# Value products of a sliding-window attention on eight TensorE tiles in place of four lanes

## The chip, the cores and the metric

The kernel runs on one core of one Trainium2 chip. The metric is the device time of one execution in microseconds (us), as the median of several runs.

## The reference

The input x has 2048 rows of 640 numbers. It is normalised (layer norm) and then used twice.

```python
qkv = (xn @ wqkv)                      # 32 heads of 20 numbers each
scores = q k^T * 20 ** -0.5            # key j counts for query i if 0 <= i - j < 256
p = softmax(scores);  o = p v
s = o @ wo
h = relu(xn @ w1 + b1) ** 2            # 640 -> 1536
g = silu(h @ w2 + b2)
out = x + s * g
```

Everything is float32. A block of 128 queries sees at most three blocks of 128 keys.

## The kernel before

All of the work after a short first stage (layer norm, the values' projection, the first keys and queries) runs in one interleaved stream whose order is written out while the program is built. It has 267 steps. A step s does three things of the attention for a pair of heads p (16 pairs) and a block of 128 rows: it makes the scores of query block s and their row maxima (`scores`, L479; `maxima`, L487, on DVE), nine steps later the transposed scores of a key block (`scores_t`, L519) and their exponentials (`exps`, L525 on ACT, then a mask on POOL, L526 and L528), and, eleven steps later and after every fourth key block, the products with the values (`values`, L547). Between these stand the dense products: keys and queries of later pairs (`qkps`), the hidden layer (`hps`) and its output (`yps`), all recorded by one helper (L469).

**Two halves.** Scores and dense products use 64 of the 128 rows of TensorE at a time, so two run side by side, one on each row half. A dense job first does the first half of its contraction on row half 0 (its front), then the rest on row half 1 (its back) into the same bank of PSUM, while the next job's front runs. Two jobs are in flight at any time, and a third bank is being emptied.

**Values.** A group is four key blocks of one pair of heads. Its products contract over 128 keys, so they take all rows, and only a quarter of TensorE's columns: head and parity of the query block pick one of four lanes, and four lanes run side by side. They are plain float32 products, while the dense ones and the scores are in the rounded float32 type. The results gather in one bank of their own, `ot`, which holds four query blocks per parity and is emptied by halves: ACT copies 256 columns to `osb` (L552) and a transfer stores it to `o_d`. The values carry a column of ones, so row 20 of each lane is the sum of the softmax.

**Banks.** Of eight banks three rotate among the dense jobs (`Acc`, `banks`), two hold scores, two the transposed scores, and one the values.

**The planner.** `clock` holds the times that the planner believes, for row half 0, row half 1 and the last one used. `COST` prices a product by its columns, `PV` a group of values. `pace` is the length of a step, from the sum of all prices. `fill(upto)` takes dense products from the generator `fl` until the clock reaches the step's end; where no bank is believed to be free, the generator gives nothing and the clock jumps. `later(wait, fn)` puts off the emptying of a bank: `SOON` after the job, and `Acc.free(after)` says when the bank may be taken again. The instructions of each engine run in the order in which they were recorded, and each waits for what it needs; the planner's clock only sets that order.

**The end.** After the last step the remaining dense work is done, then `o` is read back (`load`, L1107), divided by the sums (`invert`, `turn_out`) and multiplied with wo (`out_filler`, L607), 480 products for sixteen row blocks.

Of the kernel before, what the change touches and what calls it, by code (L numbers as in the profile page):

```python
# [19 lines left out]
H = 32  # L20
DH = 20
NT = S // P
KC = D // P
NP = H // 2
NB = 4
BT = S // NB
VW = DH + 1
NPART = 3
KR = NPART * DH
HP = P // 2  # L30
# [28 lines left out]
def attn_mlp_kernel(ctx: ExitStack, tc, x, wqkv, wo, w1, b1, w2, b2, out):  # L59
    nc = tc.nc  # L60
    PSUM = bass.MemoryType.PSUM
# [4 lines left out]
    po_ = ctx.enter_context(tc.tile_pool(name="po", bufs=1, space=PSUM))  # L66
# [346 lines left out]
    at2 = ctx.enter_context(tc.tile_pool(name="at2", bufs=2))  # L413
    stg = ctx.enter_context(tc.tile_pool(name="stgp", bufs=8))

    vps = {}

    def load_v(p):
        vp = at2.tile([P, NB, 4, 2, VW], F32, tag="vp", name=f"vp_{p}")
        nc.sync.dma_start(vp.rearrange("p b t h w -> p (b t h w)"), v_d[:, p].rearrange("p b n -> p (b n)"))  # L420
        vps[p] = vp

    clock = [0.0, 0.0, 0.0]
# [83 lines left out]
    pts = {}  # L507
# [20 lines left out]
            nc.gpsimd.affine_select(p32[:, :, 2 * P:], p32[:, :, 2 * P:], pattern=[[0, 2], [-1, P]], compare_op=ALU.is_gt, fill=0.0, base=0, channel_multiplier=1)  # L528
        pts[p, kb] = p32

    ot = po_.tile([P, 4, P], F32, tag="o", name="ops")

    def values(p, g):
        for kb in range(4 * g, 4 * g + 4):
            pt = pts.pop((p, kb))
            ts = range(kb, min(kb + 3, NT))
            same, other = [t for t in ts if t % 2 == kb % 2], [t for t in ts if t % 2 != kb % 2]
            parts = [same] if kb % 8 < 6 else [[t] for t in same]
            for part in parts + [other]:
                for hh in range(2):  # L540
                    if not part:
                        continue
                    t = part[0]
                    r0 = 32 * (2 * hh + t % 2)
                    c0 = t // 2 % 4
                    first = t % 8 < 2 and kb == max(0, t - 2) or kb == 0
                    nc.tensor.matmul(ot[r0:r0 + VW, c0:c0 + len(part), :], vps[p][:, kb // 4, kb % 4, hh, :], pt[:, hh, :].rearrange("p (t n) -> p t n", n=P)[:, t - kb:part[-1] - kb + 1:2, :], start=first, stop=part[0] == kb, skip_group_check=True)  # L547
        clock[:2] = [max(clock[:2]) + PV] * 2

        def evac():  # L550
            osb = at2.tile([P, 2, P], F32, tag="osb", name="osb")
            nc.scalar.activation(osb, ot[:, 2 * g % 4:2 * g % 4 + 2, :], AF.Copy)  # L552
            post(o_d[g][p], osb.rearrange("p e n -> p (e n)"), 0.8)
        later(SOON, evac)


# [494 lines left out]
    recs = {}  # L1051
# [3 lines left out]
    def invert():  # L1055
        for g in range(NB):
            over = state[2] >= 10 ** 6
            if not over and state[2] < stored(g) + 3:
                return
            if g not in recs:  # L1060
                rows = o_d[g].rearrange("p (h r) n -> (p h) r n", h=2)
                recs[g] = at2.tile([P, P], F32, tag="rec", name="rec")
                for par in range(2):
                    nc.sync.dma_start(recs[g][64 * par:64 * (par + 1)], rows[:, 32 * par + DH].rearrange("h (j n) -> h j n", n=P))
            elif recs[g] is not None and (state[2] >= stored(g) + 6 if not over else True):
                nc.vector.reciprocal(recs[g], recs[g])
                nc.sync.dma_start(rec_d[g].rearrange("a h (j n) -> (a h j) n", n=P), recs[g])
                recs[g] = None

    def room_of(tag, name):  # L1070
        if tag == "p32":
# [26 lines left out]
    def load(u):  # L1098
        if u in ld or u >= 2 * NB or recs.get(u // 2, 0) is not None:
            return  # L1100
        if u % 2 == 0:
            obs[u // 2] = bigp.tile([P, KC * BT], F32, tag="big", name=f"ob_{u // 2}")
        ob = obs[u // 2][:, u % 2 * 2 * D:(u % 2 + 1) * 2 * D].rearrange("p (c n) -> p c n", c=KC)
        sums = at2.tile([P, MT if u // 2 % 3 == 0 else BT], F32, tag=("sums", "relu", "sq")[u // 2 % 3], name="sums")[:, :MT]
        rows = o_d[u // 2].rearrange("p (h r) n -> (p h) r n", h=2)[:, 32 * (u % 2):32 * (u % 2) + VW]
        for k in range(4):
            nc.sync.dma_start(ob[32 * k:32 * k + H], rows[:, k:DH:4])  # L1107
# [90 lines left out]
    fl = filler()  # L1198
# [15 lines left out]
    with tc.manual_schedule(engines={E_.PE, E_.Activation, E_.DVE, E_.Pool, E_.SP}):  # L1214
        load_v(0)
        nc.vector.memset(ot, 0.0)
        loads = []

        def at_step(n):
            return divmod(n, NT) if 0 <= n < NP * NT else None  # L1220

        for s in range(steps):
            state[2] = s
            vload[0] = 0.2 * (s % 4 == 0) + 0.5 * (s % 4 == 3)
            post_all()
            invert()
            if s >= NP * NT - NT + LAG + 2:
                fetch_y()
            issue(RATE)
            a, b, e = (at_step(s - lag) for lag in (0, LAG, LAG + PLAG))  # L1230
            if a:
                p, q = a
                if q == 0:
                    ensure_bulk(loads)
                if s == 2:
                    ones_rows(1)
                if q == 2 and p < NP - 1:
                    assert made_for(p + 1, 0)
                    loads = [bulk_dma(0.7, *l) for l in pair_loads(p + 1, 0)]
                if q == LAG and p < NP - 1:  # L1240
# [58 lines left out]
```

## Time and profile before

| what | value |
|---|---|
| median of three runs | 851.08 us (850.88 to 851.49) |
| profiled execution, first to last instruction | 849.5 us |
| TensorE matmuls busy | 841.8 us (99%) |
| DVE, ACT, POOL busy | 457.9, 420.9, 330.4 us |
| value products | 2112 rows in 64 groups, from 151.8 to 767.7 us |
| granted TensorE clock | 0.999 |

The profiled execution lists its span and no other time of its own; the median of the runs is 1.6 us above it. A line of a group names the source line, engine, operation, output and inputs, the shape, the count, the busy time, the mean duration of one in ns, and the idle time of the engine ahead of them with what ended it. A line of the timeline gives the start in us, the duration, the engine and the same names; rows of the same kind that follow each other are one line. A matmul's duration is modelled and holds the time in which it passes through the array, so neighbours overlap; the distance of starts tells how long one streams. A float32 value product is recorded as two rows.

### The profile page before, as it was taken

The numbers are of one execution on the slowest core, as the hardware profiler recorded it, in microseconds if no ns is written. First come the engines' busy times: TensorE is split into PE (matmuls) and PEld (weight loads), VectorE is DVE, ScalarE is ACT, GpSimd is POOL, SyncE is SP. The second block draws the span as 40 slices with busy tenths as digits, with TensorE's granted clock in tenths as the row PEclk, the third lists the DMA queues.
The fourth block names the chain that finished last, engine by engine and source line by source line (L and its number), as shares of the span: only waits on it lengthen the run. The fifth ranks groups of instructions, "written<-read, shape, count | busy, mean of one in ns | idle before, by whom it ended". The sixth has DMA issues, their size and how long they took to land.

```text
span 849.5 us, 25542 instructions
## 1 busy us (share of the span) xinstructions
PE 841.8 (99%) x10160; PEld 784.3 (92%) x10160; DVE 457.9 (54%) x1370; ACT 420.9 (50%) x792; POOL 330.4 (39%) x652
## 2 busy tenths in 40 slices
PE   9999999999999999999999999999999999999997
PEld 8999999888888999999999999999999999999997
DVE  7653126665567645455445466755455455436753
ACT  5232114545556763664653664853763754763321
POOL 6010002434334553553552553643553543542442
PEclk9999999999999999999999999999999999999999
DMA  7997587868979565337248245576456355467993
GB/s 248 316 403 286 176 207 260 268 215 266 309 246 288 152 196 151 93 116 200 79 151 219 86 126 151 141 224 188 111 163 199 109 166 190 129 155 212 291 233 118
DMA packets 94398, 166.42 MB, mean 196 GB/s; under 512 B 10952, under 2 KB 43848, under 8 KB 93256
## 3 DMA queue, kind: packets, MB, share of 16 engines
q1 hardware_dynamic: 94120, 164.64, 63.9%
q8 instruction: 80, 1.31, 0.7%
q14 instruction: 38, 0.31, 0.1%
q10 hardware_dynamic: 160, 0.16, 0.1%
HBM read 93.66 MB, written 70.52 MB: 193 GB/s over the span
## 4 chain that ended last, share of the span: by engine, by line
PE 97%; DVE 1%; DMA 1%; issue 0%; ACT 0%; SPq 0%; DVEq 0%
PE yps L469 21%; PE hps L469 21%; PE qkps L469 14%; PE ops L547 10%; PE wops L607 8%; PE vps L229 8%; PE stps L519 5%; PE sps L479 4%; PE qkps L206 3%; PE tps L173 1%; DMA qs<-q_d 0%; DMA xt<-in_A_x_dram 0%; PE tps L302 0%; PE stps L494 0%; PE warm_ps L316 0%
## 5 line engine op out<-in xcount | busy, mean ns | idle before, releaser
L487 DVE CUSTOM_DVE_ANT_0 junk<-sps,mask 128x384 bf16<-128x384 f32 (+2 forms) x512 | 272.6, 532 | 257.7 <-PE hps L469 73.4
L525 ACT ACTIVATE p<-stps 128x768 f32<-128x768 f32 (+2 forms) x256 | 197.4, 771 | 257.2 <-PE stps L519 209.8
L526 POOL TENSOR_SCALAR_AFFINE_SELECT p<-p 128x256 f32<-128x256 f32 x256 | 110.1, 430 | 322.3 <-ACT p L525 317.0
L469 PE MATMUL yps<-w,hh 64*128 64x320 f32 x1536 | 228.3, 310 | 0.8 <-DVE ysb L996 0.7
L469 PE MATMUL hps<-xb,w 64*128 64x256 f32 (+1 forms) x2100 | 218.6, 305 | 0.0
L469 PEld LDWEIGHTS hps<-xb,w 64*128 64x128 f32 x2100 | 199.2, 187 | 6.2 <-issue 5.1
L469 PEld LDWEIGHTS yps<-w,hh 64*128 64x128 f32 x1536 | 181.9, 185 | 5.9 <-issue 3.4
L469 PE MATMUL yps<-w,hl 64*128 64x320 f32 x768 | 174.1, 309 | 0.0
L479 PE MATMUL sps<-ks,qs 60*128 60x384 f32 (+2 forms) x512 | 142.5, 340 | 0.2 <-DVE mt L487 0.2
L519 PE MATMUL stps<-qs,ks 62*128 62x384 f32 (+2 forms) x512 | 136.0, 330 | 0.1
L469 PEld LDWEIGHTS yps<-w,hl 64*128 64x128 f32 x768 | 113.7, 185 | 1.7 <-issue 1.7
L469 PE MATMUL qkps<-xT,wgkh 64*128 64x512 f32 x320 | 100.4, 395 | 0.0
L469 PE MATMUL qkps<-xT,wgqh 64*128 64x512 f32 x320 | 97.8, 392 | 0.0
L528 POOL TENSOR_SCALAR_AFFINE_SELECT p<-p 128x256 f32<-128x256 f32 x224 | 93.6, 418 | 0.0
L547 PE MATMUL ops<-p,vp 128*21 128x128 f32 (+1 forms) x2112 | 92.8, 313 | 0.0
L519 PEld LDWEIGHTS stps<-qs,ks 62*128 62x128 f32 x512 | 88.2, 187 | 1.3 <-issue 0.4
L479 PEld LDWEIGHTS sps<-ks,qs 60*128 60x128 f32 x512 | 86.2, 185 | 2.3 <-DVE mt L487 0.8
L547 PEld LDWEIGHTS ops<-p,vp 128*21 128x21 f32 x2112 | 65.2, 100 | 23.6 <-issue 11.6
L229 PE MATMUL vps<-wv,xT 128*128 128x320 f32 x480 | 71.5, 308 | 0.0
L229 PEld LDWEIGHTS vps<-wv,xT 128*128 128x128 f32 x480 | 70.5, 188 | 0.1
L966 POOL TENSOR_TENSOR hl<-sq,hh 128x512 fp32r<-128x512 f32 x48 | 62.2, 1297 | 18.9 <-ACT sq L965 18.8
L607 PE MATMUL wops<-wo,oT 128*128 128x320 f32 x384 | 61.6, 309 | 0.0
(104 smaller groups left out, 1165.0 us busy)
## 6 DMA issues: line engine op xcount, KB each, us to landing
ks<-k_d SPq DMA_DIRECT2D x64, 240.0 KB
qs<-q_d SPq DMA_DIRECT2D x64, 240.0 KB
xb<-xs SPq DMA_DIRECT2D x60, 256.0 KB
xs<-xT SPq DMA_DIRECT2D x8, 1280.0 KB
k_d<-shm SPq DMA_DIRECT2D x19, 512.0 KB
q_d<-shm SPq DMA_DIRECT2D x19, 512.0 KB
y<-ysb SPq DMA_DIRECT2D x28, 320.0 KB
o<-osb SPq DMA_DIRECT2D x64, 128.0 KB
```

The source lines that it names most:

```text
L206: nc.tensor.matmul(ps, wt[:, c, :], xT[part][b][:, c * BT + t0:c * BT + t0 + n], start=m == 1, stop=m == 3 * KC)
L229: nc.tensor.matmul(ps, xT[xp][b][:, c * BT + t * P: c * BT + (t + 1) * P], wv[wp][:, c, nh * HALF:(nh + 1) * HALF], start=first and m == 0 ...
L469: return nc.tensor.matmul(out, a[r], b_[r], skip_group_check=True, **kw)
L479: nc.tensor.matmul(ss[hh][:, :nk], qs[i][o, q * P:(q + 1) * P], ks[i][o, k0 * P:k0 * P + nk], start=True, stop=True)
L487: nc.vector.tensor_tensor_reduce(out=junk[:, :nk], in0=ss[hh][:, :nk], in1=mask[:, 3 * P - nk:], scale=1.0, scalar=-3.0e38, op0=ALU.add, o ...
L519: nc.tensor.matmul(tps[:, hh, :n], ks[i][o, kb * P:(kb + 1) * P], qs[i][o, kb * P:kb * P + n], start=True, stop=True)
L525: nc.scalar.activation(p32[:, :, :n], tps[:, :, :n], AF.Exp, scale=SCALE)
L526: nc.gpsimd.affine_select(p32[:, :, 0:P], p32[:, :, 0:P], pattern=[[0, 2], [1, P]], compare_op=ALU.is_ge, fill=0.0, base=0, channel_multip ...
L528: nc.gpsimd.affine_select(p32[:, :, 2 * P:], p32[:, :, 2 * P:], pattern=[[0, 2], [-1, P]], compare_op=ALU.is_gt, fill=0.0, base=0, channel ...
L547: nc.tensor.matmul(ot[r0:r0 + VW, c0:c0 + len(part), :], vps[p][:, kb // 4, kb % 4, hh, :], pt[:, hh, :].rearrange("p (t n) -> p t n", n=P ...
L607: nc.tensor.matmul(ps, a, b_, start=j == 0, stop=j == n - 1)
L966: nc.gpsimd.tensor_sub(hh[1][:, :BT], sq, f32(hh[0]))
```

## The change

Each value product is cut in two by the row halves, so 64 keys by 32 columns of TensorE make a tile, and there are eight tiles: two row halves, two heads, two parities of the query half block. A query half block is 64 queries. Of the six half blocks that a key block's stored probabilities cover, each key half takes five or fewer, since the window leaves one out: three of its own parity (192 columns) and two of the other (128 columns). Some are widened at a group's ends, so that every column of the bank is written.

The two row halves add up in two banks, `ops0` and `ops1`, which are taken from the dense jobs' rotation like any dense job's bank. The rotation has four banks now, since the values' own bank is gone. Ahead of a group `open_banks(2)` takes dense products, for up to 2 us of the planner's clock, until two banks are believed to be free. Afterwards ACT copies `ops0` to `osb` (up to 384 columns), DVE adds `ops1` to it, and POOL adds the last 128 columns of the group before, since a group now writes all query half blocks that its keys reach. `PV` is 1.37 in place of 1.57.

In `o_d` the two parities of half blocks now lie in different rows, so reading `o` back takes sixteen transfers of 64 columns for each part where it took four of 256, and the sums take four for two. A memset on POOL fills the values' last eleven columns once for each pair. The scratch for DMA descriptors of the kernel's builder is set to 8192.

```diff
-PV = 1.57
+PV = 1.37
     def mm_bank(shape, name):
-        turn[0] = (turn[0] + 1) % 3
+        turn[0] = (turn[0] + 1) % 4
...
     def values(p, g):
-                    nc.tensor.matmul(ot[r0:r0 + VW, c0:c0 + len(part), :], vps[p][:, kb // 4, kb % 4, hh, :], ...)
+        accs = [Acc(BT, f"ops{r}") for r in range(2)]
...
+                        lane, o = 32 * (2 * hh + odd), (kb - k0 + first // 2) * HP
+                        rows = slice(r * HP, (r + 1) * HP)
+                        nc.tensor.matmul(accs[r].tile[lane:lane + LW, o:o + n * HP], vps[p][rows, v0:v0 + LW], pt[rows, hh, first:end:2, :], ...)
         clock[:2] = [max(clock[:2]) + PV] * 2
+        def halves_meet():
+            nc.vector.tensor_add(osb[:, :cols], accs[1].tile[:, :cols], osb[:, :cols])
+            accs[1].free(0.9)
+        def carry():
+            if g:
+                nc.gpsimd.tensor_add(osb[:, :2 * HP], osb[:, :2 * HP], carried.pop(p)[:, 4 * HP:])
...
+            post(o_d[g][p], osb[:, :4 * HP], 0.8)
         def evac():
-            nc.scalar.activation(osb, ot[:, 2 * g % 4:2 * g % 4 + 2, :], AF.Copy)
-            post(o_d[g][p], osb.rearrange("p e n -> p (e n)"), 0.8)
+            nc.scalar.activation(osb[:, :cols], accs[0].tile[:, :cols], AF.Copy)
+            accs[0].free(0.9)
+            later(0.7, halves_meet)
+            later(1.5, carry)
         later(SOON, evac)
-    banks = [(0.0, j) for j in range(3)]
+    banks = [(0.0, j) for j in range(4)]
...
         for k in range(4):
-            nc.sync.dma_start(ob[32 * k:32 * k + H], rows[:, k:DH:4])
+            for odd in range(2):
+                for e in range(2):
+                    nc.sync.dma_start(to[32 * k:32 * k + H, :, e, odd], rows[:, odd, k:DH:4, e, u % 2])
...
+    def open_banks(n):
+        end = clock[0] + 2.0
+        while clock[0] < end and not (len(banks) >= n and banks[n - 1][0] <= clock[0] + 0.1):
+            c = next(fl, None)
+            if c is None:
+                clock[0] += 0.1
+            soon()
...
                 fill((s + 1) * pace - PV)
+                open_banks(2)
                 values(e[0], e[1] // 4)
```

The order of instructions moves in many places. The first is on PE behind the third group of values of pair 12 (group 51 of 64). Before, the scores of the next step (`sps`, `stps`) follow the values, and then dense output products (`yps`); the next scores come 24 dense products after these.

```order
L547 MATMUL ops<-p_11444,vp_10281 21x128 x2
L469 MATMUL yps<-w_1_1_9330,hl 128x320
L469 MATMUL yps<-w_1_1_9330,hh 128x320
L479 MATMUL sps<-ks_1351,qs_1350 128x384 [waits DVE_49] x2
L519 MATMUL stps<-qs_116,ks_117 128x256 [waits Activation_49]
L519 MATMUL stps<-qs_116,ks_117 128x256
L469 MATMUL yps<-w_1_1_9330,hh 128x320
L469 MATMUL yps<-w_1_2_9481,hh 128x320
L469 MATMUL yps<-w_1_0_9281,hl 128x320
```

In the changed kernel the same place reads as follows; `ops_12404` is the bank of the second row half.

```order
L557 MATMUL ops_12404<-p_12246,vp_11011 32x128
L470 MATMUL yps<-w_1_1_10124,hh 128x320
L470 MATMUL yps<-w_1_2_10251,hh 128x320
L480 MATMUL sps<-ks_1348,qs_1347 128x384 x2
L520 MATMUL stps<-qs_113,ks_114 128x256 [waits Activation_49]
L520 MATMUL stps<-qs_113,ks_114 128x256
L480 MATMUL sps<-ks_1348,qs_1347 128x384 [waits DVE_49]
L480 MATMUL sps<-ks_1348,qs_1347 128x384 [waits DMAHW7_49,DMAHW0_49,DVE_49]
L520 MATMUL stps<-qs_113,ks_114 128x128 [waits Activation_49]
L520 MATMUL stps<-qs_113,ks_114 128x128
L495 MATMUL stps<-ident,mt_98 64x64 x2
L470 MATMUL yps<-w_1_0_10076,hh 128x320
```

The dense products between the two steps' scores are gone from there, and the second step's scores, which wait for DVE, stand right behind the first's.

The second place is on ACT at the same group. Before, the copy of the values (`osb`) stands behind the exponential of the next step (`p` from `stps`).

```order
L525 ACTIVATE p_11545<-stps 128x768
L525 ACTIVATE p_11586<-stps 128x2x256
L552 ACTIVATE osb<-ops 128x256
L525 ACTIVATE p_11632<-stps 128x2x128
L500 ACTIVATE row<-stps 8x128
```

In the changed kernel it stands in the same place and is wider.

```order
L526 ACTIVATE p_12360<-stps 128x768
L526 ACTIVATE p_12454<-stps 128x2x256
L574 ACTIVATE osb<-ops_12403 128x384
L526 ACTIVATE p_12471<-stps 128x2x128
L501 ACTIVATE row<-stps 8x128
```

The copy did not move against the exponential: in 63 of 64 groups one exponential of the next step stands ahead of it. What is new is that a dense job's bank hangs on it. DVE's addition of `ops1` comes behind the next maxima on DVE's queue.

More of the change, by code (lines that the diff above doesn't have):

```diff
@@ L27 @@
 VW = DH + 1
+LW = 32
 NPART = 3
@@ L529, in exps @@
         pts[p, kb] = p32
-    ot = po_.tile([P, 4, P], F32, tag="o", name="ops")
+    carried = {}
     def values(p, g):
[L534 to L539, printed above, removed]
-                for hh in range(2):
[L541 to L547, printed above, removed]
-        clock[:2] = [max(clock[:2]) + PV] * 2
+        accs = [Acc(BT, f"ops{r}") for r in range(2)]
+        begun = set()
+        k0, k1 = 4 * g, 4 * g + 3
+        cols = (6 if g < NB - 1 else 4) * HP
+        for kb in range(k0, k1 + 1):
+            pt = pts.pop((p, kb)).rearrange("p h (t n) -> p h t n", n=HP)
+            there = min(6, 2 * (NT - kb))
+            for wide in (True, False):
+                for hh in range(2):
+                    for r in range(2):
+                        odd = r if wide else 1 - r
+                        first, end = r + (odd != r), min(r + 5, there)
+                        if not wide and r == 1 and kb == k0:
+                            first = 0
+                        if not wide and r == 0 and kb == k1:
+                            end = there
+                        n = len(range(first, end, 2))
+                        if not n:
+                            continue
+                        lane, o = 32 * (2 * hh + odd), (kb - k0 + first // 2) * HP
+                        rows = slice(r * HP, (r + 1) * HP)
+                        v0 = (2 * kb + hh) * VW
+                        nc.tensor.matmul(accs[r].tile[lane:lane + LW, o:o + n * HP], vps[p][rows, v0:v0 + LW], pt[rows, hh, first:end:2, :], start=(r, lane) not in begun, stop=kb == k1, skip_group_check=True)
+                        begun.add((r, lane))
+        clock[:2] = [max(clock[:2]) + PV] * 2
+        osb = at2.tile([P, 6 * HP], F32, tag="osb", bufs=3, name="osb")
+        def halves_meet():
[4 more added lines that the diff above has]
+                nc.gpsimd.tensor_add(osb[:, :2 * HP], osb[:, :2 * HP], carried.pop(p)[:, 4 * HP:])
+            if g < NB - 1:
+                carried[p] = osb
+            post(o_d[g][p], osb[:, :4 * HP], 0.8)
@@ L1060, in invert @@
             if g not in recs:
-                rows = o_d[g].rearrange("p (h r) n -> (p h) r n", h=2)
+                rows = o_rows(g)
                 recs[g] = at2.tile([P, P], F32, tag="rec", name="rec")
                 for par in range(2):
-                    nc.sync.dma_start(recs[g][64 * par:64 * (par + 1)], rows[:, 32 * par + DH].rearrange("h (j n) -> h j n", n=P))
+                    for odd in range(2):
+                        nc.sync.dma_start(recs[g][64 * par:64 * (par + 1), odd * HP:(odd + 1) * HP], rows[:, odd, DH, :, par])
             elif recs[g] is not None and (state[2] >= stored(g) + 6 if not over else True):
@@ L1068, in invert, with o_rows @@
                 recs[g] = None
+    def o_rows(g):
+        return o_d[g].rearrange("p (h b r) (e a n) -> (p h) b r e a n", h=2, b=2, e=2, a=2)
     def room_of(tag, name):
@@ L1104, in load @@
         sums = at2.tile([P, MT if u // 2 % 3 == 0 else BT], F32, tag=("sums", "relu", "sq")[u // 2 % 3], name="sums")[:, :MT]
-        rows = o_d[u // 2].rearrange("p (h r) n -> (p h) r n", h=2)[:, 32 * (u % 2):32 * (u % 2) + VW]
+        rows = o_rows(u // 2)
+        to = ob.rearrange("p c (e b n) -> p c e b n", e=2, b=2)
         for k in range(4):
-            nc.sync.dma_start(ob[32 * k:32 * k + H], rows[:, k:DH:4])
+            for odd in range(2):
+                for e in range(2):
+                    nc.sync.dma_start(to[32 * k:32 * k + H, :, e, odd], rows[:, odd, k:DH:4, e, u % 2])
         nc.sync.dma_start(sums, rec_d[u // 2][u % 2].unsqueeze(0).to_broadcast([4, H, MT]))
```

10 lines of the change are left out of this document (4 added, 6 removed).

## The prediction

> **What bounds the kernel now.** I read the page first: the busy shares, the chain that ended last, and the groups of the engines that serve the products.
>
> ```profile
> PE   9999999999999999999999999999999999999997
> ...
> PE 97%; DVE 1%; DMA 1%; issue 0%; ACT 0%; SPq 0%; DVEq 0%
> ...
> L487 DVE CUSTOM_DVE_ANT_0 junk<-sps,mask 128x384 bf16<-128x384 f32 (+2 forms) x512 | 272.6, 532 | 257.7 <-PE hps L469 73.4
> L525 ACT ACTIVATE p<-stps 128x768 f32<-128x768 f32 (+2 forms) x256 | 197.4, 771 | 257.2 <-PE stps L519 209.8
> ```
>
> TensorE never rests, and the two engines beside it sit idle waiting for it. So a change counts by two things only: how long TensorE streams, and whether it begins to wait. I then read one group of value products in the timeline, the third group of pair 12, on PE, ACT and DVE (start, duration, engine, line).
>
> ```profile
> 640.73 0.45 PE L469 MATMUL yps<-w,hh 64*128 64x320 f32 x2
> 641.10 1.50 PE L547 MATMUL ops<-p,vp 128*21 128x256 f32 x32
> 642.53 0.41 PE L469 MATMUL yps<-w,hl 64*128 64x320 f32 x1
> 642.54 0.44 PE L479 MATMUL sps<-ks,qs 60*128 60x384 f32 x1
> ...
> 644.69 0.33 PE L479 MATMUL sps<-ks,qs 60*128 60x384 f32 x1
> 644.70 0.31 PE L469 MATMUL yps<-w,hl 64*128 64x320 f32 x1
> ...
> 644.93 0.22 PE L494 MATMUL stps<-ident,mt 64*64 64x64 f32 x1
> 644.96 0.39 PE L469 MATMUL yps<-w,hh 64*128 64x320 f32 x1
> ```
>
> ```profile
> 640.64 0.81 ACT L525 ACTIVATE p<-stps 128x768 f32<-128x768 f32 x1 [1.58 <-PE stps L519]
> 643.42 0.60 ACT L525 ACTIVATE p<-stps 128x512 f32<-128x512 f32 x1 [1.98 <-PE stps L519]
> 643.92 0.38 ACT L552 ACTIVATE osb<-ops 128x256 f32<-128x256 f32 x1
> ```
>
> ```profile
> 643.16 0.56 DVE L487 CUSTOM_DVE_ANT_0 junk<-sps,mask 128x384 bf16<-128x384 f32 x1 [1.43 <-PE yps L469]
> 643.64 0.08 DVE L487 DVE_READ_ACCUMULATOR2_ANT mt<- 128x1 f32 x1
> 643.87 0.56 DVE L487 CUSTOM_DVE_ANT_0 junk<-sps,mask 128x384 bf16<-128x384 f32 x1
> 644.35 0.08 DVE L487 DVE_READ_ACCUMULATOR2_ANT mt<- 128x1 f32 x1
> ```
>
> Three things are to be seen. The values hold TensorE for 1.43 us, from 641.10 to 642.53. The copy that empties them ends at 644.30, 1.77 us after TensorE went on, because it stands behind the next step's exponential. And the maxima of the scores begun at 642.54 end at 644.43: their two banks are free 1.89 us after the scores began. Neither delay costs anything now: the values have a bank of their own, and the next scores start 2.15 us after the last.
>
> **Part 1: the streaming.** These rows keep shapes apart (mean ns of one).
>
> ```profile
> L469 PE MATMUL hps<-xb,w 64*128 64x256 f32 x1680 | 185.7, 283 | 0.0
> L469 PE MATMUL hps<-xb,w 64*128 64x512 f32 x420 | 89.4, 394 | 0.0
> L547 PE MATMUL ops<-p,vp 128*21 128x128 f32 x1344 | 88.6, 274 | 0.0
> L547 PE MATMUL ops<-p,vp 128*21 128x256 f32 x768 | 75.1, 382 | 0.0
> ...
> L547 PE MATMUL ops<-p,vp x2112: 272/273/396, 151.8 to 767.7; 128*21 128x256 f32 x96, 128*21 128x128 f32 x96
> ```
>
> A dense product grows by 111 ns for 256 columns, 0.43 ns each; a value product by 108 ns for 128, 0.84 ns each, and each shows as two rows (2112 for 1056 instructions). A lane (a quarter of the columns) gets 768 columns in a group: 768 x 2 x 0.84 ns = 1.29 us of the 1.43. After the change the busiest of the eight tiles (its key half and its queries of the same parity, three half blocks for each of four key blocks) gets 4 x 192 = 768 columns too. So eight tiles stream no shorter than four lanes did, though each does half the rows. Only a pair's last group shrinks, from 640 columns to 576: 64 x 2 x 0.84 ns = 0.11 us, 16 times, 1.7 us.
>
> What can shrink is the change of shape around a group. The last dense product before it starts at about 640.87 and streams 320 x 0.43 = 0.14 us, so the way in costs about 0.08; the way out is 1.43 - 1.29 = 0.14; together 0.22 us. Nothing in the trace runs eight such tiles; the nearest row is the small transpose L494, 64 columns wide within a row half, after which the dense row takes 0.39 us where its neighbour takes 0.31. I take 0.09 for both ways in place of 0.22: 64 x 0.13 = 8.3 us. With the 1.7 that is **-10 us**; the ends are -15.8 (no cost at all) and -1.7 (the same cost). [...] The L494 row speaks for something between.
>
> **Part 2: what TensorE waits for now.** Two of four banks belong to a group from its first product until ACT has copied the first and DVE has added the second. Three waits follow; I counted the work between the rows in TensorE's order, priced at 0.43 ns a column on each half.
>
> *Scores too soon.* The planner asks for two free banks first (up to 2 us late) and then catches up by placing steps with little or no dense work between them. In the place shown above, 24 dense products between two scores became none: the second scores come 384 + 256 columns, 0.28 us, after the first. But their banks are free only after 1.9 us. In the changed order 20 of the 64 groups are followed by such a step (0.29 to 1.09 us of work, 0.74 on average): 20 x (1.9 - 0.74) = **23 us**. Steps at 1.4 to 1.9 us add **3 us**. Before, one step lies under 1.8.
>
> *The first values' bank.* ACT's order keeps the next exponential ahead of the copy. With the usual exponential (0.81 for 0.60) and 384 columns for 256 (0.11 more, by the rows below, 0.06 for 64 columns) the bank is free 1.77 + 0.21 + 0.11 = 2.1 us after TensorE went on. In 25 of the other 44 groups the next product in that bank comes sooner, after 1.38 us of work on average: 25 x 0.72 = **18 us**. In the 20 groups with a short step that wait covers this one.
>
> ```profile
> L552 ACT ACTIVATE osb<-ops 128x256 f32<-128x256 f32 x64 | 24.2, 378 | 0.0
> L252 ACT ACTIVATE vt<-vps 128x320 f32<-128x320 f32 x16 | 7.0, 439 | 55.8 <-PE vps L229 55.8
> L885 ACT ACTIVATE shm<-qkps 128x512 fp32r<-128x512 f32 x32 | 18.9, 592 | 15.2 <-PE qkps L469 14.7
> L961 ACT ACTIVATE relu<-hps,b1t 128x256 f32<-128x256 f32 (+1 forms) x80 | 37.4, 511 | 2.2 <-PE hps L469 2.0
> L996 DVE TENSOR_TENSOR ysb<-yps,yin 128x320 f32<-128x320 f32 x32 | 15.6, 488 | 14.8 <-PE yps L469 10.3 <-issue 2.0 <-POOL p L528 1.4
> L888 DVE TENSOR_TENSOR slo<-qkps,shm 128x512 fp32r<-128x512 f32 x32 | 22.0, 688 | 9.1 <-ACT shm L885 9.0
> ```
>
> *The second values' bank.* It is one that a dense group just left, with 1.1 to 1.5 us of work in between (24 times a hidden product, 26 times an output product) or 2.1 to 2.6 (14 times queries or keys). A hidden product's bank takes 0.17 (what a row lasts beyond its stream, 283 - 111), 80/48 x 0.47 = 0.78 for ACT, and up to an exponential of 0.81 ahead of it: 0.95 to 1.76, so about 0.25 late on average, 6 us. An output product's (0.17 + 0.49 and up to one maximum of 0.64 ahead) and the keys' and queries' (0.17 + 0.59 + 0.69 and what stands between) are mostly in time; 2 us for both. **8 us**, between 0 and 20.
>
> **Part 3: the rest.** DVE gains 64 additions of 384 columns, about 0.55 us by L996 and L888; each waits in DVE's queue for ACT's copy, and behind it stand the next maxima and often a y result. I cost it at nothing because those maxima come a step later, and at 0.4 us for some 20 groups, 8 us, if they do not. ACT's 64 longer copies (0.11 each, 7 us) and POOL's 48 carries and 16 small memsets lie on engines that idle. The stores of o now wait for POOL's carry on SP's queue, with key, query and maxima transfers behind them; those are wanted steps later: nothing. The last stage reads o by 128 transfers for 32.
>
> ```profile
> 752.53 1.89 SPq L1107 DMA_DIRECT2D ob<-o  x4
> ...
> 795.00:810.00 15.00, 15.00 (x104) 15.00 (x104) 9.60 (x14) 4.61 (x7) 7.30 (x7) 1.00 1.09 268
> ```
>
> One costs SP 0.47 us, so each of eight blocks costs 5.7 us more of the queue, beside some 60 products of 0.147, 8.8 us, which TensorE runs without a gap (15.00 of 15.00). SP would have about 16 x 0.47 + 3 = 10.5 us for each 8.8: late by 1.7 for each, some six times, against a lead of a block. I take 0, at most 5.
>
> **The sum**, against this execution's span of 849.5 us: -10 + 23 + 3 + 18 + 8 = +42, so 891.5. The runs' median, 851.08, lies 1.6 above the span, which gives **893 us**.
>
> **Rivals.**
> *Faster: the waits do not come.* If what TensorE still has in its queue covers the evacuations, only part 1 is left: 851 - 10 = 841 us. For it: ACT and DVE are only half busy. Against it: the delays of 1.77 and 1.89 us are chains behind TensorE's own last scores, not load, and no idle time shortens them. 8%.
> *Slower still: the tiles do not all run side by side.* If the two of one lane take turns, a lane streams 768 + 576 columns: 576 x 2 x 0.84 ns = 0.97 us more, 64 times, +62: 955 us. If instead TensorE cannot start the pieces fast enough, the price is like it: a group is now 63 rows, and the densest train in the trace is one of 40 rows in 1.52 us, 38 ns each.
>
> ```profile
> 552.48 1.52 PE L547 MATMUL ops<-p,vp 128*21 128x256 f32 x40
> ```
>
> At that rate 63 rows take 2.4 us, 1.0 more, +64: 957 us. For it: no row of the trace shows more than four tiles at once. Against it: dense products run now side by side on the two row halves over all columns (starts 644.69 and 644.70), and the trains of 40 and of 32 rows take the same 1.5 us, so streaming and not starting sets their length. 8%. [...]
> *It does not do what it says*: waits and gain cancel within 0.2% (1.7 us, about what a measurement of this kernel can tell from no change): the waits would have to be a quarter of what I count. 2%.
>
> **How the numbers follow.** The forecast case has 82%. Half of the waits (26 us) with the gain of 15.8 gives 861; all of them with the second bank's upper end (20 for 8) and DVE's 8 us, 72 us, with a gain of 1.7 give 921. Left out are the faster, the equal and the much slower case, 18%. Faster 8%, same 2%, slower 90%.
>
> **What would show it.** Right: the group of values takes 1.35 to 1.45 us; TensorE's busy share falls to about 95%; its list of waits names ACT's copy of the values (18 us) and DVE's maxima before the scores (25 us), both now near zero; the distance of groups grows from 9.8 ((767.7 - 151.8) / 63) to about 10.4 us. Wrong: groups of values over 1.7 us mean that the tiles share something; a distance under 9.7 with no new waits means that the delays are covered. The last stage still runs without gaps on TensorE, or else SP's 96 extra transfers bind.

## The result and the profile after

| | before | changed kernel |
|---|---|---|
| median | 851.29 us (850.88 to 851.75) | 938.93 us (937.24 to 941.49) |
| span of the profiled execution | 849.5 us | 937.1 us |
| first to last start of a value product | 151.8 to 767.7 us | 150.9 to 810.9 us |
| from there to the end | 81.8 us | 126.2 us |

The ratio is 1.103, 95% interval 1.101 to 1.105. The change costs 87.6 us of span, half of it (44.0) between the first and the last values, and half (44.4) behind them. The direction was forecast, the size not: 893 us with a range to 921.

The page of the changed kernel, its first two parts and its chain:

```profile
PE 889.7 (95%) x12080; PEld 815.8 (87%) x12080; DVE 483.6 (52%) x1433; ACT 427.8 (46%) x792; POOL 352.2 (38%) x716
...
PE   8999999999999999999999999999999999969887
...
PEclk9999999999999999999999999999999999989899
...
PE 77%; DMA 6%; SPq 6%; DVE 4%; issue 4%; ACT 3%; POOL 0%; DVEq 0%; ACTq 0%
```

The chain was 97% TensorE before and is 77% now; SP's queue and DMA, which had 0 and 1%, have 12%. The row of TensorE shows holes in the last slices alone, since a slice is 23 us and hides waits of a few tenths. The list of TensorE's waits has both kinds:

```profile
PE wops L631 <- DVE res L1218: 12.9, 5, 4.7
PE sps L480 <- DVE mt L488: 7.3, 25, 0.4
PE yps L470 <- DVE ysb L1020: 6.3, 1, 6.3
PE yps L470 <- ACT osb L574: 5.7, 12, 0.8
...
PE hps L470 <- ACT osb L574: 1.6, 3, 0.8
PE qkps L470 <- ACT osb L574: 1.6, 5, 0.4
PE wops L631 <- DVE wo L830: 1.2, 1, 1.2
PE ops L557 <- ACT relu L985: 1.0, 3, 0.3
```

The maxima ahead of the scores and the copy of the values are there by name as foretold, with 7.3 and 8.9 us (5.7 + 1.6 + 1.6) in place of the 25 and 18 that were forecast for them; why the list shows less is said below. TensorE's busy share of 95% and the distance of groups, (810.9 - 150.9) / 63 = 10.5 us, are as forecast too. The two largest single waits, 6.3 and 4.7 us, are of the last stage. In front of the first of them, on SP's queue (start, duration, what is issued):

```profile
809.84 9.67 SPq L1138 DMA_DIRECT2D ob<-o  x16
819.55 0.58 SPq L1139 DMA_DIRECT2D sums<-rec  x1
820.22 1.80 SPq L804 DMA_DIRECT2D raw<-in_A_wo_dram  x4
822.13 0.37 SPq L934 DMA_DIRECT2D yin<-y  x1
```

and on TensorE:

```profile
819.72 0.31 PE L470 MATMUL yps<-w,hl 64*128 64x320 f32 x1
826.34 0.90 PE L470 MATMUL yps<-w,hh 64*128 64x320 f32 x4 [6.31 <-DVE ysb L1020]
```

A bank of `yps` is emptied by DVE, which adds `yin`. The transfer of `yin` is issued at 822.13, behind the sixteen reads of `o`, which held SP from 809.84 to 819.51. TensorE stands still until 826.34. Sixteen reads in a row held the queue for 0.60 us each (9.67 / 16) where the forecast took 0.47.

The other of the two waits, 4.7 us, shows how a late read of `o` reaches TensorE. DVE works in the recorded order, and the product that empties a bank of `wops` (`res`) stands behind the division of the next block (`ob` by `sums`). That needs the reads of `o`, which are issued until 876.05, and of the sums behind them (the profile names `yk`, issued next). SP, then DVE, then TensorE:

```profile
864.74 11.31 SPq L1138 DMA_DIRECT2D ob<-o  x16
880.91 1.56 DVE L1154 TENSOR_TENSOR ob<-ob,sums 128x512 f32<-128x512 f32 x2 [10.83 <-DMA yk<-y]
882.38 0.48 DVE L1218 TENSOR_TENSOR res<-wops,ysb 128x320 f32<-128x320 f32 x1
883.01 3.54 PE L631 MATMUL wops<-wo,oT 128*128 128x320 f32 x12 [4.67 <-DVE res L1218]
```

What follows such holes is in the windows (stretch, its length, TensorE's busy time; behind POOL the granted clock, DMA share and GB/s):

```profile
820.00:826.00 6.00, 0.03 (x1) 0.00 (x0) 1.68 (x3) 0.71 (x2) 0.00 (x0) 0.84 0.73 168
826.00:831.00 5.00, 4.66 (x30) 4.66 (x31) 3.04 (x6) 4.67 (x6) 0.00 (x0) 0.51 0.41 93
831.00:837.00 6.00, 6.00 (x57) 5.81 (x57) 0.00 (x0) 0.00 (x0) 0.00 (x0) 1.00 0.60 134
...
880.00:890.00 10.00, 6.99 (x29) 6.99 (x30) 5.30 (x8) 2.73 (x4) 3.78 (x4) 0.66 0.66 194
```

TensorE is busy for 0.03 of the 6.00 us from 820, and in the 5 us from 826 the granted clock is 0.51. The values themselves, an undisturbed group of the changed kernel and then one of before:

```profile
405.02 1.50 PE L557 MATMUL ops<-p,vp 64*32 64x192 f32 x64
406.45 0.41 PE L470 MATMUL yps<-w,hl 64*128 64x320 f32 x1
```

```profile
405.63 1.50 PE L547 MATMUL ops<-p,vp 128*21 128x256 f32 x32
407.06 0.38 PE L469 MATMUL hps<-xb,w 64*128 64x256 f32 x1
```

Both hold TensorE for 1.43 us.

The view of waits names only part of what is lost, because the two row halves run side by side (products of the two start at 406.45 and 406.46) and one may wait alone. I worked the rest out from the starts of all matmuls, counting each as streaming for 0.43 ns a column from its start. "Idle": no half streams. "One half": one does; a us of it costs half a us. "Groups": from a group's first value product to the next dense one, summed over 64. "End": from the last values' start to the end of the span.

| kernel | time | idle in the steps | one half in the steps | groups | end |
|---|---|---|---|---|---|
| before | 851.3 | 23.7 | 83.5 | 88.3 | 81.8 |
| changed | 938.9 | 55.8 | 109.4 | 96.1 | 126.2 |
| e3: reads as before | 907.1 | 58.9 | 108.9 | 96.1 | 92.3 |
| e5: and copy first | 887.1 | 38.2 | 98.3 | 93.9 | 97.7 |
| e9: e3 with four lanes | 901.5 | 57.3 | 108.4 | 91.8 | 92.3 |
| e11: one bank, copy first | 848.2 | 22.2 | 79.8 | 88.6 | 81.7 |
| e12: e11, asks for two banks | 875.5 | 42.8 | 93.2 | 88.6 | 80.2 |

In the steps the changed kernel loses 32 us of idle time, 13 of one half alone and 8 in the groups, 53 in all, and does 8 us less dense work, which lies behind the last values now. The levels of the two middle columns hang on the 0.43 ns by some us, the differences between rows by about one. Of a stretch at half the clock about half counts as idle time here: the profiled execution of e3 (mean granted clock 0.996) has two of 3.4 us in its steps (from 328.2 and 741.2 us), e9 (0.998) one, the others none, and so e3's idle time is 3 us above the changed kernel's.

### The profile page after: what moved, and what is told of

It reads as the page before. It is cut to its first block, busy times and chain, and to the rows that moved or that the text cites. A ratio compares the mean times of both kernels' runs of the same rounds, so it can differ in the third digit from the quotient of the medians.

```text
span 937.1 us, 29791 instructions
## 1 busy us (share of the span) xinstructions
PE 889.7 (95%) x12080; PEld 815.8 (87%) x12080; DVE 483.6 (52%) x1433; ACT 427.8 (46%) x792; POOL 352.2 (38%) x716
## 4 chain that ended last, share of the span: by engine, by line
PE 77%; DMA 6%; SPq 6%; DVE 4%; issue 4%; ACT 3%; POOL 0%; DVEq 0%; ACTq 0%
PE hps L470 18%; PE yps L470 17%; PE qkps L470 12%; PE ops L557 10%; PE vps L229 8%; PE sps L480 5%; PE stps L520 4%; SPq L1138 4%; PE qkps L206 3%; DVE junk L488 2%; ACT osb L574 1%; DMA ob<-o 1%; DMA yin<-y 1%; DMA out_dram<-res 1%; PE wops L631 1%
## 5 line engine op out<-in xcount | busy, mean ns | idle before, releaser
L470 PE MATMUL yps<-w,hh 64*128 64x320 f32 x1536 | 233.7, 313 | 12.2 <-DVE ysb L1020 6.3
L470 PEld LDWEIGHTS hps<-xb,w 64*128 64x128 f32 x2100 | 195.0, 186 | 10.8 <-issue 5.8
L520 PE MATMUL stps<-qs,ks 62*128 62x384 f32 (+2 forms) x512 | 126.9, 334 | 0.0
L470 PE MATMUL qkps<-xT,wgqh 64*128 64x512 f32 x320 | 101.7, 395 | 0.6 <-ACT osb L574 0.6
L557 PE MATMUL ops<-p,vp 64*32 64x192 f32 (+2 forms) x4032 | 98.7, 301 | 1.9 <-ACT relu L985 1.0
L480 PEld LDWEIGHTS sps<-ks,qs 60*128 60x128 f32 x512 | 79.7, 184 | 19.2 <-DVE mt L488 17.7
L557 PEld LDWEIGHTS ops<-p,vp 64*32 64x32 f32 x4032 | 71.8, 105 | 23.5 <-issue 11.6
L631 PE MATMUL wops<-wo,oT 128*128 128x320 f32 x384 | 69.6, 332 | 14.9 <-DVE res L1218 12.9
L520 PEld LDWEIGHTS stps<-qs,ks 62*128 62x128 f32 x512 | 78.9, 187 | 0.8
L631 PEld LDWEIGHTS wops<-wo,oT 128*128 128x128 f32 x384 | 63.2, 205 | 17.8 <-ACT oT L1155 11.5
```

Source lines behind the costliest of these rows:

```text
L470: return nc.tensor.matmul(out, a[r], b_[r], skip_group_check=True, **kw)
L480: nc.tensor.matmul(ss[hh][:, :nk], qs[i][o, q * P:(q + 1) * P], ks[i][o, k0 * P:k0 * P + nk], start=True, stop=True)
L520: nc.tensor.matmul(tps[:, hh, :n], ks[i][o, kb * P:(kb + 1) * P], qs[i][o, kb * P:kb * P + n], start=True, stop=True)
L557: nc.tensor.matmul(accs[r].tile[lane:lane + LW, o:o + n * HP], vps[p][rows, v0:v0 + LW], pt[rows, hh, first:end:2, :], start=(r, lane) not ...
```

## The experiments

**The theory**: the loss has two places. Behind the last values SP's queue binds, because sixteen transfers take the place of four. Between the steps it is the two banks. **The rivals**: the loss behind the values is the dense work pushed there, or the small pieces themselves; the loss between the steps is the new shape.

**e1 and e2: the kernel before, with its reads of o cut in four.** The one cuts the columns as the change does (256-byte pieces), the other the heads (1 KB pieces, 8 heads in each read for 32).

```diff
-            nc.sync.dma_start(ob[32 * k:32 * k + H], rows[:, k:DH:4])
+            for q in range(4):   # e1
+                nc.sync.dma_start(ob[32 * k:32 * k + H, :, q * HP:(q + 1) * HP], rows[:, k:DH:4, q * HP:(q + 1) * HP])
+            for q in range(4):   # e2
+                nc.sync.dma_start(ob[32 * k + 8 * q:32 * k + 8 * q + 8], rows[8 * q:8 * q + 8, k:DH:4])
```

> The kernel before, with each read of o cut into four reads of 64 columns (128 transfers for 32, pieces of 256 bytes for 1 KB), the same bytes to the same places. Theory, tail: SP's queue binds the last stage, 16 issues of about 0.6 us for each block against 8.8 us of products; the time grows by 25 to 40 us, to 876 to 891, all of it behind the last values. Rival, the forecast's own step: the reads are hidden, at most 5 us, up to 856.

> The kernel before, with each read of o cut into four by heads: 128 transfers for 32, but still pieces of 1 KB, so four times the issues and the same pieces. If the number of transfers on SP's queue costs the time, as much is lost as with reads of 64 columns (25 to 40 us). If the small pieces on the DMA engines cost it, under 5 us.

e1 took 885.03 us (ratio 1.040, 1.038 to 1.042), 33.9 more than before in the same series (851.17); e2 took 872.79 (1.026, 1.024 to 1.028), 21.6 more. Nothing else differs from the kernel before, so 128 reads for 32 cost some 34 us. e2 lies between its two cases (25 to 40, and under 5): about 22 us go with the number of reads and 12 more with the smaller pieces. TensorE's waits, of e1 and then of e2:

```profile
PE wops L607 <- DVE res L1188: 20.2, 7, 9.6
PE yps L469 <- DVE ysb L996: 4.3, 2, 3.6
```

```profile
PE wops L607 <- DVE res L1188: 15.5, 8, 7.1
...
PE yps L469 <- DVE ysb L996: 1.2, 2, 0.7
```

The two names are the largest of the changed kernel's last stage.

**e3: the changed kernel with the reads as before. e4: half of the reads on ACT's queue.**

```diff
-                    nc.sync.dma_start(to[32 * k:32 * k + H, :, e, odd], rows[:, odd, k:DH:4, e, u % 2])
+            nc.sync.dma_start(ob[32 * k:32 * k + H], rows[:, k:DH:4])   # e3
+                    (nc.sync, nc.scalar)[odd].dma_start(...)            # e4
```

> The changed kernel with the reads of o and of the sums as before the change: 32 transfers of 256 columns, two for the sums. It takes o in the order in which it is stored, so the columns of the blocks are mixed in the output; the amount of work is the same. Theory, tail: 30 to 40 us less than the changed kernel, 899 to 909, and what is left above before, 48 to 58, lies between the steps. Rival: under 10 us less, so the last stage is slow for another reason.

> The changed kernel with every second pair of the small reads of o issued on ACT's queue in place of SP's. Theory, SP's issue time binds: the last stage loses most of its waits, 20 to 35 us less than the changed kernel, 904 to 919. Rival, the small pieces bind on the DMA engines: within 8 us of the changed kernel.

e3 took 907.14 us (1.065, 1.064 to 1.067), 31.8 less than the changed kernel; no product of the last stage is in its list of waits, and the end is 92.3 us, of which some 8 are moved dense products. So the loss behind the values is the reads', from both sides (+34, -32). It can be added up as well: in the changed kernel's list the waits of the last stage are 12.9 + 6.3 + 1.2 us and two smaller ones, 1.0 together. The halved clock behind the holes costs some 10 more (7.9 in the last products, as worked out below, and 2.3 in the dense ones from 826.34 to 830.9, where the granted clock was 0.50). That is 31.6 in all. e4 took 922.63 (1.083, 1.080 to 1.085), 16.3 less and somewhat above its range: a second queue buys back half. The run has a price of its own: eight reads held ACT's queue for 3.9 to 10.1 us, and ACT's own work of the last stage stood behind them. With e2 this speaks for SP's issuing as the larger part of the price; how the rest divides between small pieces and ACT's delay is not shown.

**e5: e3 with ACT's copy ahead of the next exponential.**

```diff
-            accs[0].free(0.9)
-            later(0.7, halves_meet)
-            later(1.5, carry)
-        later(SOON, evac)
+            accs[0].free(SOON + 0.9)
+            later(SOON + 0.7, halves_meet)
+            later(SOON + 1.5, carry)
+        evac()
```

> The changed kernel with the reads of o and of the sums as they were before the change (o in its stored order, so that the output's columns are mixed, as in the run of that name, 907.1 us), and with ScalarE's copy of the values out of the two banks put ahead of the next step's exponential instead of behind it; where the dense work stands keeps its planner times. Theory (about 18 us of the 52 between the steps are the values' banks, which come free late because the copy stands behind an exponential): 887 to 893 us, and the gaps in front of yps, qkps and hps fall together from about 22 us to under 8, those in front of sps stay near 15. Rival (the banks' gaps are not the copy's place but the two banks that the dense products lack, so that any order of ScalarE leaves them): 903 to 909, the same gaps. Second rival (the exponential that now stands behind the copy makes the next scores late): over 909, with more in front of sps.

887.1 us (1.042, 1.041 to 1.044), 20 less, as the theory had it. The 20 are a net figure. By the table the steps lose 25 us less than the changed kernel's (idle 17.6, half of 11.1, groups 2.2), and behind the last values a new hole of 4.5 us (`ysb`, from 796.0) takes some back, as does the clock (0.995 on average in the profiled execution, 1.000 in e11's). No wait of TensorE names the copy any longer, and the scores' is as it was:

```profile
PE sps L480 <- DVE mt L488: 7.1, 23, 0.4
PE yps L470 <- DVE ysb L1020: 4.5, 1, 4.5
...
PE ops L557 <- ACT relu L985: 1.2, 3, 0.5
```

**e6, e7, e8: the short steps.** In e6 `open_banks` may take 0.5 us of the planner's clock for 2.0. In e7 a step without values lasts at least 2.1 us of it; e8 is e5 and e7 together. All three also have a way out for the planner where it would wait for ever for work that is put off (not shown); put into e3 alone, it leaves all instructions as they are. The first sentence of e6's expectation speaks of put-off subtractions; what the edit changes is the stretch in `open_banks`.

```diff
-        end = clock[0] + 2.0
+        end = clock[0] + 0.5                              # e6
-                fill((s + 1) * pace)
+                fill(max((s + 1) * pace, begun_at + 2.1))  # e7
```

> The same reads as before the change (mixed columns, 907.1 us), and the planner lets VectorE's put-off subtractions hold back dense products for 0.5 us of its clock at a step's start instead of 2.0. Theory: the planner's stretch for open banks only moves dense products within a step, so the wait of the scores does not go: 900 to 909, gaps in front of sps 12 to 17 us. Rival (that stretch is what makes the 20 short steps short, the waits of the scores are the planner's): 885 to 895, gaps in front of sps under 5 us.

> The same reads as before the change (mixed columns, 907.1 us), and a step without values may not end before 2.1 us of the planner's clock: dense products are put into the short steps until then, taken from later ones. Theory (scores follow the last scores too soon in some 20 short steps, since the dense products that stood there went elsewhere): gaps in front of sps fall from 15 us to under 5, and the time to 888 to 898. Rival (the scores wait for ScalarE's exponential or the values' banks whatever stands between them): 903 to 911, the same gaps or the same sum of gaps under other names.

> Both edits together, the copy ahead of the exponential and the floor of 2.1 us (reads as before the change, mixed columns, 907.1 us). Theory (two waits with causes of their own, which add): 868 to 878, all gaps between the steps under 15 us together. Rival (one cause behind both, the dense work with two banks less): what the two give apart does not add, 885 to 900. If all of the change's loss between the steps were these waits, the time would come to that of the kernel before, 851, plus what the dense products left behind the last values still cost.

All three theories missed; e8's rival, 885 to 900, holds. e6 took 931.3 us (1.094, 1.092 to 1.096), 24 more than e3, and the gaps within a group grew from 3.2 us (8 times) to 8.7 (27 times): without the stretch the second bank is more often still full. The groups take 11 us more together, and the time from the last values to the end grew from 92.3 to 121.6 us, with 18 us more dense work in it; the steps from the first values to the last are not longer. e7 took 916.1 (1.076, 1.073 to 1.079): the gaps in front of `sps` fell from 15.1 to 0.5 us, and others took most of their place. e8 took 887.3 (1.042, 1.041 to 1.044), the same as e5, with the scores' wait down to 0.2 us and this at its list's head:

```profile
PE stps L520 <- DMA qs<-mrow: 6.0, 2, 4.7
PE ops L557 <- DVE slo L915: 2.2, 5, 0.7
```

Lengthening the short steps only takes the dense work from elsewhere: behind the last values there are 5 us more of it in e7 than in e3, and 7 more in e8 than in e5. The wait is a symptom, and a planner's floor doesn't cure it.

**e9: e3 with the products in the shape of before.** Key blocks 1 and 4 of a group go to `ops0`, 2 and 3 to `ops1`; banks, copies and steps stay, and DVE's addition has 256 columns for 384.

```diff
+            r = int(kb not in (k0, k1))
+            for odd in range(2):
+                for hh in range(2):
+                    nc.tensor.matmul(accs[r].tile[lane:lane + LW, o:o + there // 2 * HP], vps[p][:, v0:v0 + LW], pt[:, hh, odd:there:2, :], ...)
```

> The run with the reads as before the change (907.1 us, mixed columns), with the same order of steps and the same two banks, copies and additions, but with the products themselves in the shape of before: 128 keys by 32 columns, four lanes, 768 columns each, key blocks 1 and 4 of a group into ops0, 2 and 3 into ops1 (VectorE's addition has 256 columns for 384). Only the shape differs. Theory (eight tiles stream as long as four lanes and the change of shape costs the same, so all of the loss between the steps is the banks' and none of it, nor any gain, the tiles'): 903 to 911, a group at 1.43 us. The forecast's step (eight tiles save 0.13 us in each of 64 groups): 912 to 918. Rival (the tiles themselves bring waits, by their weight loads or by products on one row half): 880 to 900.

901.5 us (1.059, 1.058 to 1.061): four lanes are 5.6 us faster than eight tiles in the same steps, a little under the theory's range and far from the forecast's step. The table shows where: the groups, 91.8 for 96.1 us, are 4.3 of it. The rest can be the clock: e3 had one more stretch of 3.4 us at half of it, and an execution of e3 with a granted clock of 1.000 took 904.89 us. An undisturbed group is the same (median 1.438 us to the next dense product),

```profile
401.96 1.51 PE L547 MATMUL ops<-p,vp 128*32 128x192 f32 x32
```

but eight tiles need `ops1` with the second product already, and 15 of 64 groups last over 1.6 us (9 in e9, none before).

**e10, e11, e12: one bank.** The products and the layout of before, in one bank out of the rotation of four, with POOL's carry. e10 copies behind the exponential, e11 ahead of it, and e12 is e11 with the planner asking for two banks. `PV` is 1.57 in all three, as before the change.

```diff
-        accs = [Acc(BT, f"ops{r}") for r in range(2)]
+        accs = [Acc(BT, "ops0")]
-                open_banks(2)
+                open_banks(1)    # e10, e11; e12 keeps open_banks(2)
```

> The values' products and the layout of o as before the change (four lanes, all rows), but their bank is one of a rotation of four, as in the change, and the planner waits for one free bank instead of two; ScalarE copies it behind the exponential, POOL adds the carried columns, VectorE adds nothing. It computes all of the reference. Theory (a group that takes two of four banks leaves the dense work too few and makes short steps; with one the four that remain are as many as before): 849 to 862. Rival (any sharing of the values' bank costs, since the dense products then wait for ScalarE's copy): 870 to 890. Second rival (the dense products gain from a fourth bank between the groups, half of TensorE's 24 us of idle time and some of its 83 us on one half alone go): 835 to 847.

> The same with one bank, and with ScalarE's copy ahead of the next exponential. It computes all of the reference. Theory (the copy's place matters as in the run with two banks, but only one bank hangs on it): 2 to 8 us under the run with the copy behind. Rival (with one bank nothing waits for the copy): the same within 2 us.

> The run with one bank and ScalarE's copy ahead of the exponential (848.2 us), with one number changed: the planner asks for two free banks ahead of a group, as in the change, though the group takes only one. Its order again has 19 steps with under 1 us of TensorE work between two scores, where the run with one bank has none. It computes all of the reference. Theory (asking for two banks is what makes the short steps, and they alone cost the 13 to 15 us in front of sps that the two-bank runs show): 861 to 872, with over 10 us of gaps in front of sps. Rival (short steps cost only where the values also hold a second bank): 847 to 853. Second rival (the asking is the whole loss between the steps, the held bank none of it): 880 to 900.

e10 took 849.08 us (0.9976, 0.9967 to 0.9986), at the lower end of the theory. e11 took 848.21 (0.9966, 0.9954 to 0.9978): faster than both kernels, by 2.9 us against before. The copy's place is worth 0.9 us there, so e11's rival holds: with one bank next to nothing hangs on it. From e9 to e10, with four lanes and the old reads in both, the second bank, its asking and DVE's addition go, and with them 52 us. e12 took 875.48 (1.029, 1.027 to 1.030), 27.3 more than e11 and 3.5 above the theory's range; neither rival fits. The waits of e11 and then of e12:

```profile
PE sps L480 <- DVE mt L488: 0.4, 2, 0.3
PE stps L520 <- ACT row L501: 0.2, 1, 0.2
```

```profile
PE sps L480 <- DVE mt L488: 9.8, 33, 0.4
...
PE stps L520 <- ACT row L501: 0.8, 1, 0.8
PE stps L520 <- ACT p L526: 0.7, 1, 0.7
```

One digit in the planner makes 19 short steps and the wait of the scores. It is a cost of the order alone: a group holds no second bank there.

## Why the prediction was wrong

**Part 3, the step that failed.** "SP would have about 16 x 0.47 + 3 = 10.5 us for each 8.8 ... I take 0, at most 5." The reads cost 32 us (e3 against the changed kernel) to 34 (e1 against before). The forecast had the right queue and the right two numbers next to each other, 1.7 us too late six times, which is 10, and then let the lead of a block swallow them. Both the number and the overlap were wrong. SP's queue went without a gap of over 0.7 us between its rows from 809.84 to 917.9 us, and from the first read of one block to the first of the next it took 13.5 us on average ((904.46 - 809.84) / 7), not 10.5. That is 4.7 above the products' 8.8, seven times, 33 us. The sixteen reads alone hold the queue for 7.9 to 11.3 us, 0.60 an issue over the eight blocks (77.2 / 128) and not 0.47, and the sums, y, x and the stores come behind them. The lead does not cover it: the first hole opens ahead of the stage's first product, since `yin` stands behind the first block's reads, and from the fifth block on the reads come too late as well.

Most holes are paid twice: 68 of the 479 distances between the last products are 0.263 us on average where 399 are 0.147, 7.9 us more, since the granted clock was 0.50 behind four of these holes (from 854.8 to 858.2, 882.1 to 888.9, 909.4 to 912.8 and 923.1 to 926.5). The range's upper end, 921, held nothing for the reads, not even the 5 us. The forecast did name the sign that came true: gaps of TensorE in the last stage mean that SP's 96 extra transfers bind.

**Part 1, the second mis-sized term.** Its count of 768 columns for lane and tile was right, and so was the 1.43 us group, inside the 1.35 to 1.45 that was to show it. But the 8.3 us for the change of shape did not come: an undisturbed group has a median of 1.435 us from its first product to the next dense one, 1.428 before. The last group of a pair got shorter, but by 0.056 us (1.159 for 1.215), 0.9 us for all sixteen and not 1.7. The small transpose, from which the forecast took its 0.09, was no measure for it. With the same 768 columns, way in and out cost the same for 128 x 32 (e9, 1.438 us) as for 64 x 32 (1.435). The term is about -1 and not -10. All groups together grew even so, 96.1 for 88.3 us: undisturbed they would take 48 x 1.435 + 16 x 1.159 = 87.4, and the other 8.7 are waits for the second bank, which part 2 has.

**Part 2 was right in its sum and in the names of its waits, and its division is shown in part only.** It counted 26 us for scores too soon, 18 for the first bank and 8 for the second, 52; the changed kernel's steps lose 53. Tried one by one: asking for two banks costs 27.3 us (e12 against e11, so in a kernel in which a group takes one bank); the copy's place 20.0 net and some 25 in the steps (e5); the groups' waits for the second bank are 8.7, and four lanes spare 4.3 of it (e9). These come to some 61 and not to 53, so they do not simply add, and neither do the edits: e8's -19.9 against e3 is not e5's -20.0 and e7's +9.0 together. That 52 met 53 so closely owes something to luck. Of the 27.3 us, 20.6 are idle time and 6.7 one row half streaming alone (e12 against e11 in the table, 13.4 halved), of which the list of waits names 9.4 (9.8 for 0.4).

**The sum.** 851 + 52 is 903, and e3 has 907. The 46 us between 893 and 939 are the reads (32), the gain that did not come (9) and some 5 of rest, of which the clock at half in e3's steps can be some 2 (904.89 us in the execution with a clock of 1.000, 907.14 in the median).

**The rivals.** All tiles run side by side: the 64 rows of a group take 1.43 us. The rate of starts that the forecast read from the train of 40 rows, 38 ns each, was no limit even before: within an undisturbed group neighbouring rows start a median of 7 ns apart there, 8 in the changed kernel. So neither the 955 nor the 957 is right, though 939 lies near them; a total near a rival is no evidence for it. The covered waits (841) are out too.

## What to carry to other kernels

A queue that needs longer for a block than the engine it feeds (here 13.5 us for 8.8) falls behind by that difference with each block, and so does everything queued behind it; count all its entries, and trust no lead that isn't in the trace. A finer tiling gained nothing here, since the busiest tile streams as many columns as before (768, and 1.43 us a group either way), and its price was paid in banks. Where a planner sets the order, try its requests apart from the work: asking for a second bank cost 27 us without using it.

## What the runs showed of the hardware

- In the changed kernel the granted clock was 0.50 from 824.1 to 830.9 us, begun within a hole of 6.31 us (from 820.03), and from 882.1 to 888.9, begun within one of 4.67 (from 878.35). Shorter holes were followed by it as well: 2.30 us ahead of 854.55 (0.50 from 854.8 to 858.2), 2.44 ahead of 908.9 (from 909.4 to 912.8) and 1.67 ahead of 921.4 (from 923.1 to 926.5). Behind holes of 1.22 us (ahead of 839.8) and 1.77 (ahead of 896.5) it stayed at 1.00. In e3, whose list of TensorE's waits has none over 0.8 us behind the first stage, the clock was halved from 328.2 to 331.6 (TensorE busy for 2.26 of the 3.00 us from 325). What decides is open.
- Eight float32 tiles of 64 x 32 ran side by side as fast as four of 128 x 32: 768 columns in the busiest tile, two rows of 0.84 ns a column for each product, 1.43 us for a group either way. The 64 rows of an undisturbed group take 22 ns each (1.43 us for all), ways in and out included, and start a median of 8 ns apart.
- Sixteen reads in a row held SP's queue for 6.94 us with 1 KB pieces of 8 heads (0.43 each, e2) and for 8.71 with 256-byte pieces of 32 heads (0.54 each, e1), in the same block of the two runs:

```profile
774.36 6.94 SPq L1108 DMA_DIRECT2D ob<-o  x16
```

```profile
779.34 8.71 SPq L1108 DMA_DIRECT2D ob<-o  x16
```
